# An H3 block with a feed-forward on one core: other pairs in seven products, another order of units, and odd butterflies first

## The chip, the cores and the metric

The kernel runs on one core of one Trainium2 chip. The metric is the device time of one execution in microseconds (us). For the kernel before, three runs gave a median of 1280.16 us (1279.25 to 1280.81). A matmul runs on PE (TensorE), element-wise work on DVE (VectorE) and ACT (ScalarE), DMAs are issued from the queues of SP (SyncE) and POOL (GpSimd).

## The reference

With q of 2048 x 1024 (S x D), w1 of 1024 x 3584 and w2 of 3584 x 1024 (D x F, F x D), all f32:

```
xn = layernorm(q)
kv = shift_conv(k, shift_k) * v                # short causal conv, 4 taps per channel
y  = irfft(rfft(kv) * rfft(ssm_k))[:2048]      # per channel, long causal conv
y  = y + kv * ssm_D
out = q + xn * y + silu(xn @ w1) @ w2
```

## The kernel before, in words

**Two matmuls of the feed-forward.** GEMM1 makes h = silu(xn @ w1), GEMM2 makes h @ w2. All operands are f16 halves, a high part and a low part of an f32 value, and a product is three matmuls for each 128 of the contraction: high by high, high by low, low by high (`steps`, L926 to L928, and `steps2`, L1054 to L1056). Splitting a value is `split` (L357): ACT writes the high part (L347), then DVE the low part (L339).

**Pairs and units.** F is cut into 14 pairs of two 128-wide column tiles. The rows of x are cut into four blocks of 512: two row halves, `sp` 0 and 1, of two blocks each. A unit is one pair and one row half. GEMM1 makes pairs 0 and 1 of the first half in the ordinary way (`plain_unit`), and every other unit by seven products instead of eight (`PRODUCTS`, L42: P1 to P7, in the order P1, P7, P6, P2, P5, P3, P4, with the next unit's P1 ahead of P3). The operands of these products are sums of blocks of x (A11, S1, ...) and of w1 (B11, T1, ...). `units` (L962) lists the units: pairs 2 to 13 of the first half, then pairs 0 to 13 of the second.

**The factors.** `factors_w1` makes the w1 operands of each pair from raw w1 by splits and DVE sums, into halves of six tiles called wo. For pairs 2 to 13 it also stores them to DRAM (`spill_w1`, tensors ws), and `load_factors` brings them back for the second half. Pairs 0 and 1 are made last, for the second half alone. `load_x` brings the x operands of the second half with transposing DMAs on SP's queue (L329) from xsp, one for each operand, as soon as the last unit of the first half has used the operand before it (`product` sets that token at pair NP - 1, the last unit of each half).

**Evacuation.** `evacuate` copies and adds the products of a unit with ACT and DVE into two row blocks, in f32, in halves of three tiles called hf, and `silu` runs on ACT. In a plain pair, `blocks` (L851) splits each row block into f16 parts in a tile ht and stores them to hs. For the pairs in `PAIRS` (10 to 13) GEMM2 uses seven products too: `quad` (L809) makes from the two row blocks seven operands, with four DVE sums of 128x512 and splits of 128x1024 (three) and 128x512 (one) and seven stores to hsf (names A.. and S..). The upper block of such a pair lies in place x4 (`room`, `parts`), the lower one in hf. There are two ht tiles.

**GEMM2.** For each of two column halves and sixteen row tiles, five chunks of four plain column tiles (`PLAIN`, L45), then `units2` with seven products for the four pairs of `PAIRS`. The w2 operands are prepared in `norms_w2`, and `load_w2` lists the loads. All operands of h come from DRAM (`load_h`).

**The long convolution.** Per group of 128 channels (eight groups) the transform is done in two stages: `stage1` does matmuls for eight residues t in four steps (`TO`, order 1, 3, 0, 2), `to_spec` (L1496) turns each step's result into a sum and a difference, `forward` (L1511) does butterflies on DVE over all eight, `product` multiplies by the filter, and stages back follow. `transforms` (L1630) runs forward for a group when steps 0 and 1 of `spec` (even and odd t) are both complete.

**What sets the order.** The program has one queue of instructions per engine. `Order` (L106) is a planner: generators yield operations with a cost and a bias, and at each step the one with the earliest due time less bias is put out. The engines then run their own lists in that order, and each waits where its next instruction's operands aren't there.

Of the kernel before, what the change touches and what calls it, by code (L numbers as in the profile page):

```python
# [13 lines left out]
F16 = mybir.dt.float16  # L14
# [25 lines left out]
            "P5": ("S1", "T1"), "P3": ("S4", "B22"), "P4": ("A22", "T4")}  # L40
XPLACE = dict(A11=2, A12=3, A22=5, S1=0, S2=6, S3=7, S4=1)

PAIRS = (10, 11, 12, 13)
NQ = len(PAIRS)
PLAIN = [j for j in range(NF) if j // 2 not in PAIRS]  # L45
NC = len(PLAIN) // 4
# [242 lines left out]
def h3_ffn_kernel(ctx, tc, x, kp, vs, fs, shift, dskip, w1, w2, cfwd, cinv, out):  # L289
# [75 lines left out]
    dram = ctx.enter_context(tc.tile_pool(name="dram", bufs=1, space=bass.MemoryType.DRAM))  # L365
    hsf = [{p[0]: dram.tile([4, P, NQ, 2, P], F16, name=f"hsf{p[0]}{b}") for p in PRODUCTS.values()} for b in range(2)]
    hs = [dram.tile([4, P, NF, 2, P], F16, name=f"hs{b}") for b in range(4)]
    ws = {i: {n: dram.tile([P, 2, KH, len(n) * P], F16, name=f"ws{i}_{n[0]}") for n in FACTORS} for i in range(2, NP)}
    xsp = {p[0]: dram.tile([P, 4, KH, 2, P], F16, name=f"xsp{p[0]}") for p in PRODUCTS.values()}

    ps_ff = ctx.enter_context(tc.tile_pool(name="ps_ff", bufs=1, space=bass.MemoryType.PSUM))
# [373 lines left out]
    def factors_w1():  # L745
        for n, (kind, i) in enumerate(pairs):
            yield (0.21, 0.15, 0.1, 0.05)[min(n, 3)]
            yield flag["scaled", n]
            hv, toks, _ = raws[n]
            b = {(a, j): hv[a][:, :, j * P:(j + 1) * P] for a in range(2) for j in range(2)}  # L750
            if kind == "plain":
                for j in range(2):
                    if i == 0:
                        yield (0.21, 0.18)[j]
                    for a in range(2):
                        yield from w_part(("plain", i, a, j), b[a, j], i)
                toks[0].set()
                continue
            sp = 0 if i > 1 else 1
            keep = ws.get(i, defaultdict(lambda: None))  # L760

            def part(names, src):
                spill = keep[names] is not None
                o, tok = yield from w_place(len(names), 1 + spill)
                yield from split(o[:, 0], o[:, 1], src, wsc[:, i, 0:1])
                factors_there(sp, i, names, o, tok)
                if spill:
                    spills.append((keep[names], o, tok, len(names)))
            yield from part(("B11",), b[0, 0])
            yield t1_r.ready  # L770
            t1, t1k = t1_r.tile([P, KH, P])
            yield v_tt(t1, b[0, 1], b[0, 0], SUB)
            yield v_tt(b[0, 1], b[1, 1], b[0, 1], SUB)
            yield v_tt(b[0, 0], b[0, 1], b[0, 0], ADD)
            yield from part(("T2", "T3"), hv[0])
            yield from part(("B21", "B22"), hv[1])
            yield from part(("T1",), t1)
            t1k.set()
            yield v_tt(b[1, 0], b[1, 0], b[0, 0], SUB)
            toks[0].set()  # L780
            yield from part(("T4",), b[1, 0])
            toks[1].set()
        flag["w done"].set()
        flag["spills end"].set()
# [10 lines left out]
                tok.set()  # L795

    def load_factors():
        for i in range(2, NP):
            for names in FACTORS:
                o, tok = yield from w_place(len(names))  # L800
                yield L(o, ws[i][names])
                factors_there(1, i, names, o, tok)
        flag["factors"].set()
# [148 lines left out]
    def product(n, i, sp, o, first=False):  # L952
        xname, wname = PRODUCTS[n]
        yield flag["w", sp, i, wname]
        yield flag["x", sp, xname]
        w, tok = wops[sp, i, wname]
        yield from steps(o, w, xo[sp][xname], first, True, not first)
        tok.set()
        if i == NP - 1:
            xtok[sp][xname].set()  # L960

    def units():  # L962

        todo = [(i, 0) for i in range(2, NP)] + [(i, 1) for i in range(NP)]
        yield ff.ready
        one = ff.tile([P, 4, P])
        yield from product("P1", *todo[0], one[0], True)
        for n, (i, sp) in enumerate(todo):
            if sp == 1:
                flag["unit", i].set()  # L970
                flag["room", 1].set()
            if i in PAIRS:
                add(quad(i, sp), 0.1)
            made, seen = defaultdict(Token), defaultdict(Token)
            yield ff.ready
            c = ff.tile([P, 4, P])
            add(evacuate(i, 2 * sp, one, c, made, seen), EB)
            yield from product("P7", i, sp, c[0], True)
            yield seen["P1"]
            two = seen["bank"][0]  # L980
            yield from product("P6", i, sp, two)
            made["P6"].set()
            yield from product("P2", i, sp, one[0])
            made["P2"].set()
            yield seen["P6"]
            yield from product("P5", i, sp, two)
            made["P5"].set()
            if n + 1 < len(todo):
                yield ff.ready
                one = ff.tile([P, 4, P])  # L990
                yield from product("P1", *todo[n + 1], one[0], True)
            yield seen["P5"]
            yield from product("P3", i, sp, two)
            made["P3"].set()
            yield seen["P7"]
            yield from product("P4", i, sp, c[0])
            made["P4"].set()
# [330 lines left out]
    def convolution(floor):  # L1328
# [130 lines left out]
        def stage1():  # L1459

            for g in range(NG):
# [4 lines left out]
                for t in TO:  # L1466
                    yield flag["part", g, t]
                    (hi, htok), (lo, ltok) = part.pop((g, t))
                    two = []
                    for i in range(2):  # L1470
                        for c in range(2):
                            if i == 0:
                                yield lambda: ps_r.ready() or spare()
                                ps, tok = (ps_r if ps_r.ready() else ff).tile([P, 2, 2 * P])
                                two.append((ps, Token(), Token(), Token()))
                                diff = (tmp[:, :, t // 2] if t % 2 else sp[:, :, 5 + t])[:, :, c]
                                add(to_spec(g, t, sp[:, :, t, c, :], diff, *two[c], tok), CB)
                            ps, seen, made = two[c][:3]
                            if i == 1:
                                yield seen  # L1480

                            def mm():
                                cf = cfw[:, t + 4 * i, :, c * P:(c + 1) * P]
                                kw = dict(skip_group_check=i == 1)
                                nc.tensor.matmul(ps, cf[:, 0], hi[:, i], start=i == 0, stop=False, **kw)
                                nc.tensor.matmul(ps, cf[:, 0], lo[:, i], start=False, stop=False, **kw)
                                nc.tensor.matmul(ps, cf[:, 1], hi[:, i], start=False, stop=True, **kw)
                            yield T(mm, ps, [hi[:, i], lo[:, i]], 0.65, m=1.0)
                            (made if i else two[c][3]).set()
                    htok.set()  # L1490
                    ltok.set()
# [4 lines left out]
        def to_spec(g, t, total, diff, ps, seen, made, half, tok):  # L1496

            yield half
            if g > 0:
                yield flag["taken", g - 1, t]  # L1500
                if t % 2 == 0:
                    yield flag["taken", g - 1, t + 1]
            yield a_act(diff, ps, AF.Copy, 2.0)
            seen.set()
            yield made
# [5 lines left out]
        def forward(g):  # L1511
# [16 lines left out]
            def I2(a, step):  # L1528
                return C(a, 2, step)[:, :, :, 1, :]

            yield v_tt(C(4, 2, 2), C(0, 2), C(2, 2), SUB)
            yield v_tt(C(2, 2), C(0, 2), C(2, 2), ADD)
            yield v_tt(C(0), C(2), C(3), ADD)
            yield v_tt(C(1), C(2), C(3), SUB)
            yield v_tt(pair(R(2), I(3)), pair(R(4), I(4)), pair(I(6), R(6)), ADD)
            yield v_tt(pair(I(2), R(3)), pair(I(4), R(4)), pair(R(6), I(6)), SUB)
            yield v_tt(pair(R(4), I(6)), pair(R(5), I(5)), pair(I(7), R(7)), ADD)
            yield v_tt(pair(I(4), R(6)), pair(I(5), R(5)), pair(R(7), I(7)), SUB)
            yield v_tt(R2(5, 2), R2(8, 1), I2(8, 1), ADD)
            yield v_tt(I2(5, 2), I2(8, 1), R2(8, 1), SUB)  # L1540
            yield v_tt(pair(R(8), R(9)), pair(R(5), I(5)), pair(I(7), R(7)), ADD)
            yield v_tt(pair(I(8), I(9)), pair(I(5), I(7)), pair(R(7), R(5)), SUB)
            for o, s, t, r in ((5, 8, 4, RT), (4, 8, 4, -RT), (7, 9, 6, RT), (6, 9, 6, -RT)):
                flat = [C(a)[:, :, 0].rearrange("p s c w -> p s (c w)") for a in (o, s, t)]
                yield v_stt(flat[0], flat[1], r, flat[2], MUL, ADD)
            tok.set()
# [82 lines left out]

        def transforms():  # L1630
            for g in range(NG):
                yield flag["spec", g, 0]
                yield flag["spec", g, 1]
                yield from forward(g)
                yield from product(g)
                add(result_scales(g), CB)
                yield from inverse(g)
# [173 lines left out]
```

## Time and profile before

| quantity | before |
|---|---|
| median of three runs | 1280.16 us |
| span of the profiled execution | 1279.8 us |
| PE busy | 1244.7 us (97%) |
| DVE busy | 1146.4 us (90%) |
| ACT busy | 725.5 us (57%) |
| POOL busy | 133.0 us (10%) |
| DMA, mean | 222 GB/s |

The profile is of one execution of 17054 instructions, whose own span is the second row; the page gives no other time for it. The share of an engine is its busy time over that span. Matmuls on PE are pipelined, so their durations overlap, and a step of time in the kernel is read from the starts. Where an engine is idle, the row says whose work it waited for. Positions are in us from the start of the span: GEMM1 ends near 613, the convolution's last DVE work is at about 1256.

### The profile page before, as it was taken

To read this page: it belongs to the slowest core of one execution; us is meant where nothing else is said; L and a number is where in the kernel's file an instruction comes from. 1 tells how busy PE (TensorE), PEld (TensorE's weight loads), DVE (VectorE), ACT (ScalarE), POOL (GpSimd) and SP (SyncE) were. 2 spreads that over 40 slices of the span, in tenths; PEclk is the share of its full clock that TensorE was granted. 3 is DMA by queue.
4 is the path that set the end of the run, shared out by engine and by line. 5 is a ranking of instruction groups with operands and counts; after the bars stand their busy time and mean duration, and the time that the engine had idled before them with its cause. 6 is when DMAs were issued, how large, how long until landed. Compare 5 with 4: busy or idle time off the path is not lost. (4 is left out here: it accounts for less than half of the span.)

```text
span 1279.8 us, 17054 instructions
## 1 busy us (share of the span) xinstructions
PE 1244.7 (97%) x6082; PEld 604.2 (47%) x6082; DVE 1146.4 (90%) x1521; ACT 725.5 (57%) x1153; POOL 133.0 (10%) x141
## 2 busy tenths in 40 slices
PE   7899999989899999999999999999999999999997
PEld 6444444434344544445444544544454454445443
DVE  8999997889699969999899899899979989997991
ACT  6858896768566687559652632553253274445231
POOL 0000000000000020002010310210030030113223
PEclk9899999989999999999999999999999999999999
DMA  9447899889999899669995684598486487877766
GB/s 329 157 150 237 284 321 307 269 241 248 290 365 356 277 282 334 225 197 261 351 290 125 138 226 111 124 254 266 107 189 180 113 170 225 228 148 142 158 127 92
DMA packets 247988, 284.53 MB, mean 222 GB/s; under 512 B 43744, under 2 KB 162528, under 8 KB 246624
## 3 DMA queue, kind: packets, MB, share of 16 engines
q1 hardware_dynamic: 221168, 258.54, 63.6%
q0 software_dynamic: 26736, 24.92, 14.6%
q8 instruction: 47, 0.77, 0.2%
q14 instruction: 37, 0.30, 0.1%
HBM read 185.88 MB, written 98.57 MB: 222 GB/s over the span
## 5 line engine op out<-in xcount | busy, mean ns | idle before, releaser
L1054 PE MATMUL ff<-x,wo 128*128 128x512 f16 x864 | 327.4, 379 | 1.4 <-ACT hf L347 1.0
L1056 PE MATMUL ff<-x,wo 128*128 128x512 f16 x864 | 327.4, 379 | 0.0
L1055 PE MATMUL ff<-x,wo 128*128 128x512 f16 x864 | 327.4, 379 | 0.0
L926 PE MATMUL ff<-x,wo 128*128 128x512 f16 (+1 forms) x808 | 306.1, 379 | 8.6 <-ACT hf L347 3.8
L927 PE MATMUL ff<-x,wo 128*128 128x512 f16 (+1 forms) x808 | 306.0, 379 | 2.6 <-DVE x L339 2.6
L928 PE MATMUL ff<-x,wo 128*128 128x512 f16 (+1 forms) x808 | 306.0, 379 | 2.5 <-DVE wo L339 2.4
L336 DVE TENSOR_TENSOR spec<-spec 128x512 f32<-128x512 f32 (+2 forms) x256 | 260.6, 1053 | 2.8 <-DVE spec L336 0.5
L1056 PEld LDWEIGHTS <-wo 128*128 128x128 f16 x864 | 84.5, 98 | 101.9
L1055 PEld LDWEIGHTS <-wo 128*128 128x128 f16 x864 | 84.5, 98 | 100.8 <-issue 2.4
L1054 PEld LDWEIGHTS <-wo 128*128 128x128 f16 x864 | 85.4, 99 | 98.7
L928 PEld LDWEIGHTS <-wo 128*128 128x128 f16 x808 | 79.7, 99 | 101.8 <-issue 5.8
L926 PEld LDWEIGHTS <-wo 128*128 128x128 f16 x808 | 81.4, 101 | 92.2 <-ACT wo L347 3.4
L927 PEld LDWEIGHTS <-wo 128*128 128x128 f16 x808 | 79.7, 99 | 95.6 <-issue 9.1
L347 ACT ACTIVATE hf<-ff,invc 128x512 f32<-128x512 f32 x64 | 43.5, 680 | 118.9 <-PE ff L1056 86.8
L333 POOL DMA_DIRECT2D out<-yt x64 | 74.5, 1362 | 338.5 <-DVE yt L339 220.9
L333 POOL DMA_DIRECT2D out<-hf x63 | 57.4, 911 | 457.9 <-ACT hf L347 391.8
L336 DVE TENSOR_TENSOR tmp<-spec 128x2048 f32<-128x2048 f32 (+1 forms) x48 | 92.5, 1933 | 1.0
L347 ACT ACTIVATE spec<-spec 128x1024 bf16<-128x1024 f32 x32 | 33.8, 1055 | 86.1 <-DVE spec L336 86.0
L339 DVE SCALAR_TENSOR_TENSOR ht<-hf,wsc,ht 128x1024 f16<-128x1024 f32 (+1 forms) x56 | 67.3, 1204 | 13.7 <-ACT ht L347 13.7
L347 ACT ACTIVATE ht<-hf,wsc 128x1024 f16<-128x1024 f32 (+1 forms) x56 | 60.5, 1083 | 11.4 <-DMA hsfS<-ht 6.9
L339 DVE SCALAR_TENSOR_TENSOR wo<-raw,wsc,wo 128x512 f16<-128x512 f32 (+1 forms) x56 | 56.1, 1012 | 9.0 <-ACT wo L347 9.0
L339 DVE SCALAR_TENSOR_TENSOR acc<-kin,taps,acc 128x1024 f32<-128x1024 f32 x48 | 61.4, 1280 | 2.2 <-ACT acc L347 2.2
(181 smaller groups left out, 1750.1 us busy)
## 6 DMA issues: line engine op xcount, KB each, us to landing
wo<-hs SPq DMA_DIRECT2D x160, 256.0 KB, 3.6
hs<-ht SPq DMA_DIRECT2D x80, 256.0 KB, 5.6
out<-hf POOLq DMA_DIRECT2D x63, 256.0 KB, 4.5
raw<-in_w SPq DMA_DIRECT2D x28, 512.0 KB, 5.8
wraw<-in_w SPq DMA_DIRECT2D x24, 512.0 KB, 6.3
w2n<-in_w SPq DMA_DIRECT2D x24, 512.0 KB, 6.8
kin<-in_kp SPq DMA_DIRECT2D x16, 704.0 KB, 6.1
xt<-in_x SPq DMA_DIRECT2D x16, 512.0 KB, 7.4
```

Source lines behind the costliest of these rows:

```text
L333: return Op("POOL", 1.1, 3.0, lambda: nc.gpsimd.dma_start(o, i, accum_op=ADD), [i], [o], m, n)
L336: return V(lambda: nc.vector.tensor_tensor(o, a, b, op=op), o, [a, b], **k)
L339: return V(lambda: nc.vector.scalar_tensor_tensor(o, a, s, b, op0=op0, op1=op1), o, [a, b] + ([] if isinstance(s, float) else [s]), **k)
L347: nc.scalar.activation(o, i, func, scale=scale, **kw)
L926: nc.tensor.matmul(o, w[:, 0, k], xf[:, :, k, 0], start=first and k == 0, stop=False, **kw)
L927: nc.tensor.matmul(o, w[:, 0, k], xf[:, :, k, 1], start=False, stop=False, **kw)
L928: nc.tensor.matmul(o, w[:, 1, k], xf[:, :, k, 0], start=False, stop=last and k == KH - 1, **kw)
L1054: nc.tensor.matmul(po, hx[:, n, 0, :], wc[:, n, 0, :], start=first and n == 0, stop=False, **kw)
L1055: nc.tensor.matmul(po, hx[:, n, 0, :], wc[:, n, 1, :], start=False, stop=False, **kw)
L1056: nc.tensor.matmul(po, hx[:, n, 1, :], wc[:, n, 0, :], start=False, stop=last and n == 3, **kw)
```

## The change

Three things are changed. First, `PAIRS` are 8 to 11 instead of 10 to 13, so that pairs 12 and 13 are plain. Second, the units come from a list `UNITS`: the first half has pairs 2 to 13 as before, the second begins with pair 13, then 0, 1, 2 to 12. Pair 13's factors are made once, are not stored to DRAM, and stay in wo until the second half's unit has used them; the loads of factors therefore start at pair 2 and end at 12. Tokens that stood at the last pair of a half now stand at the last of `UNITS[sp]`, and the flags "unit" are numbered by place in the second half. Third, in a convolution group the four butterflies on odd t come first, when the odd steps are complete, and the butterflies on even t wait for the even ones; the tiles that hold the differences are shifted by one place so that an even step no longer needs two places of the group before.

```diff
-PAIRS = (10, 11, 12, 13)
+PAIRS = (8, 9, 10, 11)
+UNITS = [[*range(2, NP)], [NP - 1, 0, 1, *range(2, NP - 1)]]
...
-    ws = {... for i in range(2, NP)}
+    ws = {... for i in range(2, NP - 1)}
...
             def part(names, src):
                 spill = keep[names] is not None
-                o, tok = yield from w_place(len(names), 1 + spill)
+                both = i == NP - 1
+                o, tok = yield from w_place(len(names), 1 + spill + both)
                 yield from split(o[:, 0], o[:, 1], src, wsc[:, i, 0:1])
                 factors_there(sp, i, names, o, tok)
+                if both:
+                    factors_there(1, i, names, o, tok)
...
     def load_factors():
-        for i in range(2, NP):
+        for i in UNITS[1][3:]:
...
     def product(n, i, sp, o, first=False):
...
-        if i == NP - 1:
+        if i == UNITS[sp][-1]:
             xtok[sp][xname].set()
...
     def units():
-        todo = [(i, 0) for i in range(2, NP)] + [(i, 1) for i in range(NP)]
+        todo = [(i, sp) for sp in range(2) for i in UNITS[sp]]
...
-                flag["unit", i].set()
+                flag["unit", n - len(UNITS[0])].set()
...
-                                diff = (tmp[:, :, t // 2] if t % 2 else sp[:, :, 5 + t])[:, :, c]
+                                diff = (tmp[:, :, t // 2] if t % 2 else sp[:, :, 4 + t])[:, :, c]
...
         def to_spec(g, t, total, diff, ps, seen, made, half, tok):
             yield half
             if g > 0:
                 yield flag["taken", g - 1, t]
-                if t % 2 == 0:
-                    yield flag["taken", g - 1, t + 1]
...
         def forward(g):
...
-            yield v_tt(C(4, 2, 2), C(0, 2), C(2, 2), SUB)
-            yield v_tt(C(2, 2), C(0, 2), C(2, 2), ADD)
-            yield v_tt(C(0), C(2), C(3), ADD)
-            yield v_tt(C(1), C(2), C(3), SUB)
-            yield v_tt(pair(R(2), I(3)), pair(R(4), I(4)), pair(I(6), R(6)), ADD)
-            yield v_tt(pair(I(2), R(3)), pair(I(4), R(4)), pair(R(6), I(6)), SUB)
-            yield v_tt(pair(R(4), I(6)), pair(R(5), I(5)), pair(I(7), R(7)), ADD)
-            yield v_tt(pair(I(4), R(6)), pair(I(5), R(5)), pair(R(7), I(7)), SUB)
+            yield flag["spec", g, 1]
             yield v_tt(R2(5, 2), R2(8, 1), I2(8, 1), ADD)
             yield v_tt(I2(5, 2), I2(8, 1), R2(8, 1), SUB)
             yield v_tt(pair(R(8), R(9)), pair(R(5), I(5)), pair(I(7), R(7)), ADD)
             yield v_tt(pair(I(8), I(9)), pair(I(5), I(7)), pair(R(7), R(5)), SUB)
-            for o, s, t, r in ((5, 8, 4, RT), (4, 8, 4, -RT), (7, 9, 6, RT), (6, 9, 6, -RT)):
+            yield flag["spec", g, 0]
+            yield v_tt(C(5, 2, 2), C(0, 2), C(2, 2), SUB)
+            yield v_tt(C(2, 2), C(0, 2), C(2, 2), ADD)
+            yield v_tt(C(0), C(2), C(3), ADD)
+            yield v_tt(C(1), C(2), C(3), SUB)
+            yield v_tt(pair(R(2), I(3)), pair(R(5), I(5)), pair(I(7), R(7)), ADD)
+            yield v_tt(pair(I(2), R(3)), pair(I(5), R(5)), pair(R(7), I(7)), SUB)
+            yield v_tt(pair(R(5), I(7)), pair(R(4), I(4)), pair(I(6), R(6)), ADD)
+            yield v_tt(pair(I(5), R(7)), pair(I(4), R(4)), pair(R(6), I(6)), SUB)
+            for o, s, t, r in ((4, 8, 5, -RT), (5, 8, 5, RT), (6, 9, 7, -RT), (7, 9, 7, RT)):
...
         def transforms():
             for g in range(NG):
-                yield flag["spec", g, 0]
-                yield flag["spec", g, 1]
                 yield from forward(g)
```

More of the change, by code (lines that the diff above doesn't have):

```diff
@@ L367, in h3_ffn_kernel @@
     hs = [dram.tile([4, P, NF, 2, P], F16, name=f"hs{b}") for b in range(4)]
-    ws = {i: {n: dram.tile([P, 2, KH, len(n) * P], F16, name=f"ws{i}_{n[0]}") for n in FACTORS} for i in range(2, NP)}
+    ws = {i: {n: dram.tile([P, 2, KH, len(n) * P], F16, name=f"ws{i}_{n[0]}") for n in FACTORS} for i in range(2, NP - 1)}
     xsp = {p[0]: dram.tile([P, 4, KH, 2, P], F16, name=f"xsp{p[0]}") for p in PRODUCTS.values()}
```

## The prediction

> **What bounds the kernel now.** First the page's list of engines and the table by stretches of 32 us (columns: wall time, then busy time and instructions of PE, PEld, DVE, ACT, POOL, then the granted clock, DMA share, GB/s).
>
> ```profile
> PE 1244.7 (97%) x6082; PEld 604.2 (47%) x6082; DVE 1146.4 (90%) x1521; ACT 725.5 (57%) x1153; POOL 133.0 (10%) x141
> ```
> ```profile
> 192.00:224.00 32.00, 32.00 (x152) 14.59 (x150) 25.17 (x36) 22.02 (x30) 0.95 (x1) 1.00 0.90 307
> 224.00:256.00 32.00, 30.64 (x144) 13.79 (x143) 25.68 (x42) 25.48 (x39) 0.00 (x0) 1.00 0.81 269
> 256.00:288.00 32.00, 28.40 (x123) 12.50 (x122) 28.15 (x46) 20.90 (x30) 0.00 (x0) 0.89 0.81 241
> 288.00:320.00 32.00, 31.63 (x152) 14.93 (x151) 29.30 (x41) 26.40 (x39) 0.00 (x0) 1.00 1.06 248
> 320.00:352.00 32.00, 27.51 (x119) 11.87 (x117) 22.25 (x24) 16.43 (x27) 0.76 (x1) 0.95 1.04 290
> 352.00:384.00 32.00, 30.28 (x141) 13.67 (x140) 31.00 (x29) 21.65 (x37) 0.00 (x0) 1.00 1.06 366
> ...
> 1248.00:1280.00 32.00, 22.70 (x117) 11.14 (x114) 5.08 (x7) 4.02 (x6) 11.03 (x11) 0.94 0.67 91
> ```
> ```profile
> 384.00:704.00 320.00, 320.00 (x1561) 153.56 (x1559) 297.65 (x360) 206.94 (x328) 24.61 (x24) 1.00 0.87 270
> 704.00:1248.00 544.00, 542.12 (x2686) 264.29 (x2685) 501.88 (x587) 234.04 (x400) 94.90 (x98) 1.00 0.70 171
> ```
>
> PE is busy all of 384 to 704 and 542.12 of the 544 us behind it, while DVE works 297.65 of 320 and 501.88 of 544: near the bound, but not it. From 384 on only the end can be won. Matmuls, ACT and DVE instructions keep their numbers under the change, so the time moves only by stalls of PE. They lie in 224 to 384: idle 1.36, 3.60, 0.37, 4.49 and 1.72 us (32 less PE busy), and where the granted clock is 0.89 and 0.95, another 0.11 and 0.05 of 32 us, 3.5 and 1.6. So the first half's end (224 to 288) loses about 8.5 us, and the second half's start (288 to 384) 8.2.
>
> Whom PE waited for between 224 and 384, and the matmuls at the longest wait:
>
> ```profile
> PE ff L926 <- ACT hf L347: 3.8, 2, 2.9
> PE ff L926 <- ACT wo L347: 2.9, 1, 2.9
> PE ff L928 <- DVE wo L339: 2.0, 3, 0.7
> PE ff L926 <- DVE hf L336: 1.7, 1, 1.7
> ```
> ```profile
> 272.23 0.38 PE L927 MATMUL ff<-x,wo 128*128 128x512 f16 x1
> ...
> 273.09 0.38 PE L928 MATMUL ff<-x,wo 128*128 128x512 f16 x1
> 276.37 0.61 PE L926 MATMUL ff<-x,wo 128*128 128x512 f16 x1 [2.90 <-ACT wo L347]
> 276.77 0.63 PE L927 MATMUL ff<-x,wo 128*128 128x512 f16 x1
> ```
>
> The wait on wo is pair 13's first factor, which comes late. Behind it a matmul takes 0.61 to 0.63 us where one took 0.38, and starts lie 0.40 apart (276.37 to 276.77) instead of 0.215 (the four from 272.23 to 273.09); at 0.215 a product of twelve matmuls takes 2.6. The wait of 2.9 on hf is an evacuation, and its cause stands in ACT's and SP's rows:
>
> ```profile
> 315.49 0.59 ACT L347 ACTIVATE ff<-ff 128x512 f32<-128x512 f32 x1
> ...
> 318.76 1.14 ACT L347 ACTIVATE wo<-raw,wsc 128x1024 f16<-128x1024 f32 x1
> 324.64 0.72 ACT L347 ACTIVATE ht<-hf,wsc 128x512 f16<-128x512 f32 x1 [4.74 <-DMA hsfS<-ht]
> ```
> ```profile
> 282.98 4.70 SPq L329 DMA_TRANSPOSE x<-xspA  x1
> 287.77 0.53 SPq L324 DMA_DIRECT2D ws_T<-wo  x1
> ...
> 302.13 6.57 SPq L329 DMA_TRANSPOSE x<-xspS  x1
> 308.79 1.08 SPq L324 DMA_DIRECT2D hsfS<-ht  x2
> 309.97 5.81 SPq L329 DMA_TRANSPOSE x<-xspA  x1
> 315.88 4.55 SPq L329 DMA_TRANSPOSE x<-xspS  x1
> 320.52 1.08 SPq L324 DMA_DIRECT2D hsfS<-ht  x2
> 321.69 6.12 SPq L329 DMA_TRANSPOSE x<-xspS  x1
> ...
> 329.08 5.48 SPq L329 DMA_TRANSPOSE x<-xspA  x1
> ```
>
> These are seven transposing loads of x from 282.98 to 334.56 (the last starts at 329.08), four of xspS and three of xspA, each holding SP for 4.55 to 6.57 us, with fifteen other transfers among them, nine of these hsf stores. The stores that would free an ht tile stand behind two of them (309.97 to 320.52), ACT stops 4.74 us at the next split, and PE's evacuation is queued behind that split.
>
> **The change part by part.** All DVE prices come from these groups of 196 to 384 (mean ns after the busy time):
>
> ```profile
> L339 DVE SCALAR_TENSOR_TENSOR ht<-hf,wsc,ht 128x1024 f16<-128x1024 f32 x12 | 15.4, 1281 | 7.5 <-ACT ht L347 7.5
> L339 DVE SCALAR_TENSOR_TENSOR acc<-kin,taps,acc 128x1024 f32<-128x1024 f32 x12 | 15.3, 1279 | 0.0
> L336 DVE TENSOR_TENSOR hf<-ff,hf 128x512 f32<-128x512 f32 x18 | 12.3, 685 | 0.1
> L336 DVE TENSOR_TENSOR x<-hf,x 128x512 f32<-128x512 f32 x4 | 2.8, 688 | 0.0
> L339 DVE SCALAR_TENSOR_TENSOR ht<-hf,wsc,ht 128x512 f16<-128x512 f32 x4 | 3.0, 751 | 4.2 <-ACT ht L347 4.2
> ```
>
> *1. Pairs 8 to 11 as quads, first half.* A quad costs DVE three splits of 1.281, one of 0.751 and four sums of 0.688: 7.35 us. A plain pair costs two splits, 2.56. In before's order, quads 10 and 11 (and 12) stand among the last factors; now 8, 9, 10 and 11 do. Ahead of pair 13's factors DVE thus gets two quads more, 2 x 4.79 = 9.6 us. DVE's idle time in 192 to 256 was 64 − 50.85 = 13.15 us, nominally enough. But half of it, by my estimate, is forced: DVE waits there for products that PE has yet to make and can do nothing early. Bounds: 0 (all hidden) to +9.6 (none). If 6.6 us are usable, 3.0 are late. Against this, the small waits on DVE's wo (2.0 in three) move: one at pair 11 goes, pair 12's grows. I take +1.5, nearer to 0, because the old loss of 8.5 already holds one such wait with its clock loss, and the new lateness adds to it rather than making a new one.
>
> *2. Second half starts with pair 13.* In the changed order the seven transposes have two loads of raw, four hs stores and one kf load among them; in before, the fifteen named above. The five stores of ws13 and their loads go:
>
> ```profile
> ws_T<-wo SPq DMA_DIRECT2D x24, 256.0 KB, 5.1
> wo<-ws_T SPq DMA_DIRECT2D x24, 256.0 KB, 7.3
> ```
>
> A store held SP for 0.53 us (287.77). They feed no instruction that PE waits for, so removed they are worth nothing themselves. What counts is the 8.2 us: with no quad store behind a transpose, ACT's 4.74 us stop has no cause. Units 13 and 0 are plain, and their four hs stores can still stand behind a transpose of up to 6.57 us, but there are two ht tiles and a plain pair takes only two splits per unit where a quad takes four. I leave 1.5 us of the 8.2 (a wait of the 1.72 kind, without clock loss): −6.7. Bounds: 0 (the transposes hold whatever store comes) to −8.2. The cost: pair 13's factors stay in wo through another 18 us (seven products of 2.6 us). Pair 0's are needed by the same 18 us later, so this nearly cancels; T4 of pair 0 waits for the wo tile that P6 of pair 13 frees, and comes close: 0 to +1, inside the bounds.
>
> *3. Second half ends with a plain pair behind a quad.* Order on DVE from the last quad's first sums on: four sums, S3/S1's split, S2/S4's split, the gate's acc, two splits of w2, and only then the last unit's evacuation of P5 into a half of hf, for which P4 of pair 12 waits. hf has three wholes; the lower block's whole is released by the S3/S1 split. That list is 4 x 0.688 + 4 x 1.281 + 1.279 + 0.685 = 9.84 us. PE does in the same time P5 (it is at work when the list starts, some 1.6 us of it left by my estimate), the copy out (0.59, as ACT's ff<-ff copies) and P3 (2.6). P3 waits about 1.0 with no next P1 to cover the copy, P4 is due 1.6 + 1.0 + 2.6 = 5.2 us in, and would wait up to 4.6; I take 3.3, since DVE in 384 to 704 ran with 22.35 us idle and can be somewhat ahead. Behind GEMM2's start one norm of the gate, whose sums queue behind this list, I price at 1.7 (0 to 2.8). Sum +6.0. Bounds: 0 (before's row has PE busy 320 of 320) to +9.8.
>
> *4. Odd butterflies alone.* The four wide subtractions and sums on even indices no longer hold the four odd ones: DVE starts sooner in each of eight groups. DVE's waits there:
>
> ```profile
> DVE spec L336 <- ACT spec L347: 30.3, 16, 3.9
> ```
>
> At most 30.3 us of DVE waiting go, 3.8 a group. But PE, not DVE, is full from 384 on (1.88 us idle in 704 to 1248), so I take 0. Bounds: −1.9 to +1.9: ACT's to_spec copies compete with evacuations either way.
>
> *5. Tail.* The last unit2 starts when the weights and products are there, as before; DVE is busy 5.08 of the last 32 us, so an earlier conv end brings nothing: 0.
>
> Sum: +1.5 − 6.7 + 6.0 + 0 + 0 = +0.8 on the execution's span of 1279.8, 1280.6. The runs' median (1280.16) is 0.36 above that span: **1281.0**.
>
> On the clock one rule bears on new waits. The Trainium skill, "TensorE: Matmul & The Clock Gate", Part 1, says that PE falls to half clock after an idle window of about 3.4 us and needs about as long a busy one to come back. By this trace a wait of 2.90 us is already enough, and that of 1.72 us was not (352 to 384 kept 1.00). By that rule none of the waits that I take for the changed kernel (3.3 at most) would cost clock, and the sum stays; by the trace it may not, which is rival C.
>
> **The rivals.**
> *A, the gain stays:* new work in 1 and 3 hides in DVE's idle 13.15 and 22.35 us. For: those idle sums are larger than 9.6 and 9.84. Against: DVE's idle comes in waits, not in one piece. Time: 1281.0 − 1.5 − 6.0 = 1273.5; with the whole 8.2 gone, 1272.0.
> *B, slower: the quad list ahead of the last plain unit and ahead of pair 12's factor holds PE for 3 us or more each.* Price: 3 at its 4.6 + 1.0 + 2.8 = 8.4, and 1 at 3.0 + one more spell at half clock (3.5, as in 256 to 288): 6.5. With −6.7: +8.2, 1288.4. It decides once DVE runs level with PE, without a lead of over 2 us, when each list starts. For: DVE busy 29.30 and 31.00 of 32 around such quads. Against: 320 to 352 had 9.75 idle.
> *C, the clock alone:* sizes as in the forecast, but each wait of 2.9 or more (3.3 in part 3, pair 12's about 3) brings a spell of half clock: 1.6 to 3.5 each by the rows of 320 and 256. Time: 1281.0 + 1.6 to 7.0, about 1284.6. For: the wait of 2.90 us was followed by half clock both times. Against: it takes waits in one piece, and those of part 3 may come in two.
> *D, part 2 doesn't do it:* hs stores stand behind the transposes as hsf's did, 8.2 stays: 1281.0 + 6.7 = 1287.7.
>
> **How the numbers follow.** Runs tell 0.2%, about 2.6 us, from no change: faster is below 1277.6, slower above 1282.7. Forecast (the terms nearly cancel, own range 1277 to 1285): 0.40, of it 0.06 faster, 0.20 same, 0.14 slower. A: 0.25, faster. B: 0.17, C: 0.10, D: 0.08, slower but for 0.02 of C. So faster 0.31, same 0.22, slower 0.47. The range 1272 to 1288 leaves out A's lower edge and B's and D's upper.
>
> **What would show it.** Part 1: PE's wait for ACT wo near 276 stays near 3 us, one near 257 appears. Part 2: in 288 to 384 the granted clock stays 1.00 and "ACT ht <- DMA hsf" is gone there. Part 3: PE waits for DVE hf between 600 and 640. Part 4: fewer us of DVE spec <- ACT spec, and no change of PE in 704 to 1248. Wrong would be: PE full in 600 to 640 (then A), a long wait in 288 to 384 (then D), or a clock below 1.00 at a third place (then C).

## The result and the profile after

| | before | after |
|---|---|---|
| median of ten runs, us | 1280.11 (1279.25 to 1281.08) | 1283.23 (1281.69 to 1285.12) |
| span of the profiled execution, us | 1279.8 | 1281.7 |
| ratio, 95% interval | | 1.0026 (1.0016 to 1.0035) |

The changed kernel is slower by 0.26%, 3.1 us. The parts are much larger than this sum. The table by stretches of the changed kernel (wall time, then busy time and instructions of PE, PEld, DVE, ACT, POOL, then granted clock, DMA share, GB/s) stands beside that of before:

```profile
224.00:256.00 32.00, 29.33 (x139) 13.32 (x138) 30.07 (x50) 27.17 (x41) 0.00 (x0) 1.00 0.92 299
256.00:288.00 32.00, 27.43 (x117) 11.82 (x115) 29.09 (x46) 20.26 (x29) 0.00 (x0) 0.89 0.81 241
288.00:320.00 32.00, 32.00 (x158) 15.59 (x156) 26.28 (x33) 24.96 (x37) 0.00 (x0) 1.00 1.06 244
320.00:352.00 32.00, 32.00 (x150) 14.46 (x148) 29.08 (x31) 20.54 (x32) 0.76 (x1) 1.00 0.83 220
352.00:384.00 32.00, 31.84 (x154) 15.08 (x153) 31.55 (x38) 23.95 (x41) 0.00 (x0) 1.00 1.04 363
384.00:576.00 192.00, 191.49 (x947) 93.07 (x946) 182.24 (x228) 137.41 (x221) 14.18 (x13) 1.00 0.88 275
576.00:608.00 32.00, 28.54 (x138) 13.34 (x137) 30.85 (x31) 24.41 (x39) 5.25 (x5) 1.00 0.99 283
608.00:640.00 32.00, 28.84 (x128) 12.79 (x128) 31.00 (x36) 19.39 (x31) 0.00 (x0) 0.95 0.98 317
640.00:704.00 64.00, 63.06 (x323) 31.77 (x322) 60.65 (x72) 32.98 (x53) 7.79 (x9) 1.00 0.64 171
704.00:1248.00 544.00, 542.09 (x2674) 262.81 (x2672) 481.39 (x563) 219.55 (x377) 97.39 (x101) 1.00 0.72 174
```

What PE lost in each stretch, in us, is counted for every kernel below as for the prediction: wall time less PE's busy time, and the part of the clock that wasn't granted. The rows of 384 to 704 of before show 0.

| stretch | before | after | change | prediction |
|---|---|---|---|---|
| 224 to 288, end of the first half | 8.5 | 10.8 | +2.3 | +1.5 |
| 288 to 384, start of the second | 8.2 | 0.2 | −8.0 | −6.7 |
| 384 to 576 | 0 | 0.5 | +0.5 | 0 |
| 576 to 640, end of GEMM1 | 0 | 8.2 | +8.2 | +6.0, for the whole end |
| 640 to 704 | 0 | 0.9 | +0.9 | |
| 704 to 1248, GEMM2 | 1.9 | 1.9 | 0 | 0 |

The sum is +3.9; the two spans differ by 1.9, since the clock is given in hundredths, half-speed matmuls overlap, and the executions differ by about 1 us in their first 64 us too. The waits of PE in the changed kernel, over the whole span, are these (total, times, longest):

```profile
PE ff L932 <- DVE wo L340: 4.6, 3, 2.6
PE ff L930 <- DVE hf L337: 4.4, 2, 3.9
...
PE ff L930 <- ACT wo L348: 2.7, 1, 2.7
...
PE ff L1059 <- DVE x L340: 1.9, 1, 1.9
```

The wait on ACT wo is still pair 13's first factor. The one of 2.6 on DVE wo is new, pair 12's, at 252. The wait of 2.9 on an evacuation has gone from 324, and one of 3.9 stands at the end of GEMM1: P4 of pair 12 waits for DVE's sum in hf. DVE's list ahead of that sum and PE's two waits, in order of time:

```profile
599.85 0.68 DVE L337 TENSOR_TENSOR hf<-hf 128x512 f32<-128x512 f32 x1
600.45 1.28 DVE L340 SCALAR_TENSOR_TENSOR x<-wraw,tau,x 128x1024 f16<-128x1024 f32 x1
601.64 0.68 DVE L337 TENSOR_TENSOR hf<-x,hf 128x512 f32<-128x512 f32 x1
602.25 1.27 DVE L340 SCALAR_TENSOR_TENSOR x<-w2n,tau,x 128x1024 f16<-128x1024 f32 x1
603.44 0.68 DVE L337 TENSOR_TENSOR x<-hf,x 128x512 f32<-128x512 f32 x1
604.16 0.69 DVE L337 TENSOR_TENSOR x<-x 128x512 f32<-128x512 f32 x1
604.77 1.28 DVE L340 SCALAR_TENSOR_TENSOR ht<-hf,wsc,ht 128x1024 f16<-128x1024 f32 x1
605.96 1.28 DVE L340 SCALAR_TENSOR_TENSOR acc<-kin,taps,acc 128x1024 f32<-128x1024 f32 x1
607.16 1.28 DVE L340 SCALAR_TENSOR_TENSOR ht<-x,wsc,ht 128x1024 f16<-128x1024 f32 x1
608.35 0.68 DVE L337 TENSOR_TENSOR hf<-ff,hf 128x512 f32<-128x512 f32 x1
```
```profile
602.47 0.38 PE L930 MATMUL ff<-x,wo 128*128 128x512 f16 x1 [0.69 <-ACT hf L348]
...
609.09 0.58 PE L930 MATMUL ff<-x,wo 128*128 128x512 f16 x1 [3.87 <-DVE hf L337]
```

Here is the list that the prediction added up: four sums and two splits of the last quad, with w2's splits and a step of the gate among them, then the evacuation. It takes 599.85 to 609.03, 9.2 us (estimated 9.84). P3 starts 2.6 us into it, just as the forecast had it (1.6 us of P5 left, then a wait of 1.0), so P4 comes 3.87 us too late, and its first matmuls run at half clock (0.58 to 0.63 us a matmul). The list is full without a gap: DVE is behind, it doesn't wait. On SP no store of quad operands stands among the transposing loads any more:

```profile
303.52 1.08 SPq L325 DMA_DIRECT2D hs<-ht  x2
304.69 5.21 SPq L330 DMA_TRANSPOSE x<-xspA  x1
310.00 4.85 SPq L330 DMA_TRANSPOSE x<-xspS  x1
```

### The profile page after: what moved, and what is told of

Its sections match the earlier page's. It is cut to its first block, busy times and chain, and to the rows that moved or that the text cites. A ratio compares the mean times of both kernels' runs of the same rounds, so it can differ in the third digit from the quotient of the medians.

```text
span 1281.7 us, 17018 instructions
## 1 busy us (share of the span) xinstructions
PE 1242.7 (97%) x6082; PEld 603.3 (47%) x6082; DVE 1144.8 (89%) x1521; ACT 725.9 (57%) x1153; POOL 133.0 (10%) x141
## 4 chain that ended last, share of the span: by engine, by line
PE 59%; DVE 22%; issue 7%; DMA 7%; ACT 4%; POOL 1%; SPq 0%; POOLq 0%; DVEq 0%; ACTq 0%
PE ff L932 9%; PE ff L930 9%; PE ff L931 9%; PE ff L1058 7%; PE ff L1060 7%; PE ff L1059 7%; DVE spec L337 6%; DVE tmp L337 3%; DVE acc L340 2%; DVE x L340 2%; PE ps L1489 2%; DVE wo L340 2%; PE ps L1491 2%; PE ps L1490 2%; DVE ht L340 1%
## 5 line engine op out<-in xcount | busy, mean ns | idle before, releaser
L334 POOL DMA_DIRECT2D out<-yt x64 | 71.7, 1346 | 349.0 <-DVE yt L340 225.3
L348 ACT ACTIVATE spec<-ps 128x512 f32<-128x512 f32 x84 | 48.7, 590 | 24.0 <-PE ps L1491 22.4
L337 DVE TENSOR_TENSOR spec<-tmp 128x512 f32<-128x512 f32 (+1 forms) x80 | 61.0, 793 | 0.8
```

Of the source, the lines that this page charges most:

```text
L334: return Op("POOL", 1.1, 3.0, lambda: nc.gpsimd.dma_start(o, i, accum_op=ADD), [i], [o], m, n)
L337: return V(lambda: nc.vector.tensor_tensor(o, a, b, op=op), o, [a, b], **k)
L348: nc.scalar.activation(o, i, func, scale=scale, **kw)
```

## The experiments

The theory after the result was that the three parts do what the stretches suggest: the pairs alone remove 288 to 384, and a plain pair behind the last quad costs the end of GEMM1. Each run below is set beside runs of before on its chip; times are medians in us.

**Each part alone, and the change without its butterflies.** E1 has only this edit:

```diff
-PAIRS = (10, 11, 12, 13)
+PAIRS = (8, 9, 10, 11)
```

> Only the pairs that take seven products are changed (8 to 11); units and butterflies as before. Theory: the 9 us that went between 288 and 384 went because no store of quad operands stands behind the transposing loads any more, and that comes from the pairs alone; the first half's end costs 2 more, and near 575 to 613 two plain pairs stand behind the last quad, for 3 to 9 us. Sum -4 to +2 on before: 1276 to 1282, with granted clock 1.00 in 288 to 384 and no ACT wait on hsf there. Rival (the order of units and the kept factors gave the 9): the loss of 8 to 9 us in 288 to 384 stays, sum +5 to +11: 1285 to 1291.

Measured: 1309.6, ratio 1.0234 (1.022 to 1.0248). Both expectations are missed. The stretch of 288 to 384 loses 0.8, 8.6 + 3.5 (clock 0.89) and 0: 12.9 us, but not by quad stores. ACT's row shows why, and PE's stretches at both places:

```profile
341.11 1.06 ACT L347 ACTIVATE wraw<-wraw 128x1024 f32<-128x1024 f32 x1 [9.47 <-DMA wraw<-in_w]
```
```profile
320.00:352.00 32.00, 23.45 (x99) 10.00 (x98) 14.40 (x18) 17.57 (x30) 0.76 (x1) 0.89 1.01 289
...
576.00:608.00 32.00, 25.76 (x118) 11.97 (x117) 31.72 (x41) 20.00 (x27) 0.00 (x0) 0.93 0.66 208
608.00:640.00 32.00, 19.30 (x95) 10.33 (x94) 24.77 (x28) 24.94 (x39) 9.71 (x9) 0.82 1.00 253
```

A load of w2, put on SP's queue behind the last transposing load, arrives late, and ACT stands 9.47 us in front of its square with the conv copies queued behind. The end of GEMM1 loses 6.2 + 2.2 and 12.7 + 5.8, 26.9 us, a loss that only E11 reaches again. PE's longest waits there are 6.2 us of a convolution matmul for ACT and 6.7 us of GEMM1 for a DVE sum in hf. The butterflies of before are in this kernel, so such a loss doesn't need those of the change. No run takes it apart, and its cause is open.

E2 is the order of units and the kept factors alone:

```diff
+UNITS = [[*range(2, NP)], [NP - 1, 0, 1, *range(2, NP - 1)]]
...
+                if both:
+                    factors_there(1, i, names, o, tok)
```

> Only the order of units is changed, with pair 13's factors kept; pairs 10 to 13 take seven products and the butterflies are as before. Theory: quads 12 and 13 still store among the transposing loads, so 288 to 384 loses 6 to 10 us as before, and the end of GEMM1 has a quad last and loses nothing: 1279 to 1283. Rival (the order of units gave the gain): 288 to 384 loses under 2 us, 1270 to 1273. Second rival (the new order costs at the end of GEMM1 whatever the pairs): 4 us or more lost in 576 to 640, 1284 to 1289.

Measured: 1286.46, ratio 1.0051 (1.0038 to 1.0065). ACT's waits between 280 and 384, and a stretch of PE:

```profile
ACT ht L348 <- DMA hsfA<-ht: 8.6, 2, 5.7
```
```profile
288.00:320.00 32.00, 30.90 (x150) 14.73 (x148) 24.08 (x33) 23.48 (x36) 0.00 (x0) 1.00 1.05 230
320.00:352.00 32.00, 27.68 (x120) 12.18 (x120) 25.51 (x30) 19.21 (x27) 0.76 (x1) 0.95 0.86 223
352.00:384.00 32.00, 30.68 (x142) 13.69 (x140) 28.81 (x30) 18.56 (x31) 0.00 (x0) 1.00 0.91 307
```

The start of the second half loses 1.1 + 4.3 + 1.3 + 1.6 = 8.3, as before, with ACT behind hsf stores (another 4.7 us behind those of S operands): the theory's half of this is right, the order of units alone wins nothing there. The second rival is right as well, though: the end of GEMM1 loses 1.1 + 4.1 us with a quad last, and the time is over the theory's 1283. So the two parts win the 8 us only together: the pairs take the quad stores out from among the transposing loads, and with the order of units the loads that ACT needs next come later. The first load of w2 is issued at 335.39 in E1, right behind the transposing loads, and at 347.75 in the changed kernel, where ACT's longest wait for such a load between 280 and 384 is 2.5 us and PE's waits come to 0.2.

E3 is the changed kernel with the `forward`, `to_spec` and `transforms` of before.

> The change without its butterflies: pairs 8 to 11 and the new order of units, butterflies as before. Theory: the 8.6 us lost in 576 to 640 come from the plain pair behind the quad and stay; some 1 us of small waits of stage1's matmuls in 640 to 1248 goes: 1281 to 1283.5. Rival (the butterflies that begin sooner crowd DVE at the end of GEMM1): 3 us or less lost in 576 to 640, 1275 to 1278.

Measured: 1278.27, ratio 0.9984 (0.9975 to 0.9992), faster than before and 5.0 us below the changed kernel. The rival is right about the end of GEMM1 (0.6 us lost), where the theory falls; its time is missed by 0.3. The rows of E3, PE's stretches first, then DVE's list (its first and last) and PE's first matmul of the same P3:

```profile
576.00:608.00 32.00, 31.74 (x170) 16.57 (x169) 31.90 (x36) 26.48 (x36) 4.39 (x4) 1.00 0.99 276
608.00:640.00 32.00, 31.62 (x154) 14.77 (x153) 28.16 (x26) 22.50 (x38) 7.03 (x7) 1.00 1.04 309
704.00:1248.00 544.00, 537.02 (x2668) 262.29 (x2667) 496.02 (x579) 233.83 (x400) 97.13 (x100) 1.00 0.71 170
```
```profile
582.34 0.69 DVE L337 TENSOR_TENSOR hf<-hf 128x512 f32<-128x512 f32 x1
...
590.86 0.68 DVE L337 TENSOR_TENSOR hf<-ff,hf 128x512 f32<-128x512 f32 x1
```
```profile
589.12 0.38 PE L930 MATMUL ff<-x,wo 128*128 128x512 f16 x1 [0.26 <-ACT hf L348]
```

The plain pair stands behind the quad here too, and the list is as long (582.34 to 591.54, 9.2 us), but it starts 6.8 us ahead of P3 instead of 2.6, and P4, which follows 2.6 us behind P3's start, doesn't wait: the sum is there 0.2 us ahead of it. What differs is DVE's lead, the time by which its list starts ahead of the product on PE. The butterflies of the change also do something in GEMM2: without them 704 to 1248 loses 7.0 us, with them 1.9. Of the 7.6 us that they cost at the end of GEMM1 they give 5.1 back. These sums are of one execution each; the two profiled ones differ by 3.3 us, the medians by 5.0.

E4 is the butterflies alone, in the kernel before.

> Only the butterflies are changed. Theory: PE is the bound behind 384, so within 1.5 us of before: 1279 to 1282, PE losing 9 us again in 288 to 384 and under 0.5 in 576 to 640. Rival (they crowd DVE): 3 us or more lost in 576 to 640, 1283 to 1289. Second rival (they shorten the convolution and with it the end): 1276 or less.

Measured: 1293.26, ratio 1.0106 (1.0087 to 1.0124). None of the three: the end of GEMM1 loses only 1.9 (608 to 640), but the stretches behind it lose:

```profile
640.00:704.00 64.00, 61.47 (x294) 28.73 (x293) 63.13 (x70) 27.08 (x42) 4.76 (x6) 1.00 0.73 201
704.00:1248.00 544.00, 537.99 (x2677) 262.84 (x2676) 488.30 (x572) 229.88 (x398) 99.42 (x102) 1.00 0.72 173
```

2.5 in 640 to 704 and 6.0 in 704 to 1248. The same butterflies that spare GEMM2 5 us beside the new pairs and units cost it 4 beside the old ones. Why is open.

**Is it the plain pair, or DVE's lead?** E5 leaves the changed kernel's work as it is and puts the quads' work of the second half ahead in the planner's order:

```diff
+    QB = (0.1, 1.0)
...
-        add(factors(("S3", "S1"), flat[1], (ltok,)), 0.1)
+        add(factors(("S3", "S1"), flat[1], (ltok,)), QB[sp])
...
-        add(factors(("S2", "S4"), flat[0], (utok, flag["quads", sp])), 0.1)
+        add(factors(("S2", "S4"), flat[0], (utok, flag["quads", sp])), QB[sp])
...
-                add(quad(i, sp), 0.1)
+                add(quad(i, sp), QB[sp])
```

> The changed kernel, in whose second half alone the quads' work goes ahead of other work in the order (bias 1.0 instead of 0.1). Theory of DVE's lead: the 8.6 us in 576 to 640 are lost because the last quad's sums and splits stand on DVE behind convolution work that the butterflies brought forward; put ahead, under 2 us are lost there and the time is 1274 to 1278. Rival (a plain pair behind a quad costs it whatever stands ahead): 5 us or more stay, 1281 to 1284.

Measured: 1272.23, ratio 0.9932 (0.9919 to 0.9946). The theory of the lead holds, and the gain is larger than it said:

```profile
576.00:608.00 32.00, 32.00 (x170) 16.53 (x169) 30.43 (x37) 28.61 (x44) 7.17 (x7) 1.00 0.96 271
608.00:640.00 32.00, 32.00 (x150) 14.52 (x149) 31.90 (x28) 20.24 (x32) 4.23 (x5) 1.00 1.06 331
704.00:1248.00 544.00, 543.55 (x2693) 264.93 (x2692) 487.89 (x571) 227.21 (x390) 101.84 (x105) 1.00 0.71 173
```

PE loses nothing from 576 to 640 and 0.45 in GEMM2, with the same work on every engine. The last quad's sums now start at 586.95, 13.5 us ahead of P3 (600.41), and the sum that P4 needs is done at 600.40, 4.5 us ahead of P4 (604.94). E6 tries the rival directly, with pair 12 put ahead of the quads:

```diff
-UNITS = [[*range(2, NP)], [NP - 1, 0, 1, *range(2, NP - 1)]]
+UNITS = [[*range(2, NP)], [NP - 1, 0, 1, *range(2, 8), 12, *range(8, 12)]]
```

> The changed kernel, with pair 12 placed behind pair 7 in the second half, so that it ends with the quads 8 to 11 and no plain pair stands behind a quad there. Rival of e5 (a plain pair behind a quad is the cause): under 1.5 us lost in 576 to 640, 1274 to 1277. Theory of DVE's lead: the lack of lead meets the last quads instead, 4 to 7 us stay, 1279 to 1283.

Measured: 1282.84, ratio 1.0019 (1.001 to 1.0027). The rival falls:

```profile
576.00:608.00 32.00, 29.77 (x131) 13.08 (x130) 31.90 (x33) 26.92 (x44) 3.05 (x3) 0.95 1.08 324
608.00:640.00 32.00, 30.17 (x143) 13.92 (x142) 31.79 (x37) 16.84 (x21) 1.57 (x2) 1.00 0.99 312
```

2.2 + 1.6 + 1.8 = 5.7 us stay in 576 to 640 with no plain pair behind a quad. So a plain pair isn't needed for a loss of this size. That DVE's lead is the cause here too isn't shown: the wait of 2.2 is for ACT's copy into hf, and only the 1.8 are waits for DVE, for an operand of GEMM2. E7 is E5's edit with the butterflies of before.

> As the kernel with the quads' work first, but with the butterflies of before. Theory: once the end of GEMM1 has its lead, the butterflies are worth nothing either way, since PE is the bound: within 2 us of the kernel with the quads first, 1274 to 1278. Rival (they cost in GEMM2 too, or they gain there): 4 us or more apart.

Measured: 1275.32, ratio 0.9964 (0.9951 to 0.9976), 3.1 above E5: more than the theory's 2, less than the rival's 4, and it is the butterflies of the change that gain. In its profiled execution (1278.69 us), PE loses 2.0 in 576 to 640, 1.0 in 640 to 704 and 2.9 in 704 to 1248 (541.15 of 544 busy). With the quads' work first, the butterflies of the change are thus worth some 3 us.

**The end of the first half.** E8 adds to E5 an earlier place for the last factors:

```diff
-            yield (0.21, 0.15, 0.1, 0.05)[min(n, 3)]
+            yield (0.21, 0.15, 0.1, 0.05)[min(n, 3)] if n < 12 else 0.1
```

> As the kernel with the quads' work first, and in the first half the factors of pairs 12 and 13 (and of 0 and 1) get the bias of the quads (0.1 instead of 0.05). Theory: the 10.5 us lost in 224 to 288 are factors that stand on DVE behind the quads' work; with the same bias the wait of 2.7 us for pair 13's first factor and the half clock behind it go, 3 to 6 us: 1269 to 1273. Rival (the factors are late for the scales or the raw loads, not for DVE's order): within 1.5 us of the kernel with the quads first.

Measured: 1278.31, ratio 0.9986 (0.9975 to 0.9998), 6.1 above E5: both times are missed. The theory's mechanism is there, and the gain is lost at the next place:

```profile
256.00:288.00 32.00, 29.77 (x132) 13.18 (x133) 31.44 (x50) 22.63 (x33) 0.00 (x0) 0.95 0.84 243
...
320.00:352.00 32.00, 27.02 (x124) 11.95 (x123) 26.27 (x29) 16.83 (x25) 0.76 (x1) 1.00 0.74 179
```
```profile
338.70 1.06 ACT L348 ACTIVATE hi<-kf 128x1024 bf16<-128x1024 f32 x1 [7.01 <-DMA kf<-in_dskip]
```

224 to 288 loses 1.4 + 2.2 + 1.6 = 5.2 instead of E5's 10.8, but the load of kf now stands behind the last transposing load instead of ahead of two, and ACT waits 7.01 us for it. 288 to 352 loses 6.1 where E5 loses nothing, and 704 to 1248 loses 3.0 where E5 loses 0.45. E9 takes E5 and moves the quads of the first half instead, `QB = (0.2, 1.0)`.

> As the kernel with the quads' work first in the second half (bias 1.0), and in the first half with a bias of 0.2 instead of 0.1. Theory: the first half's 10.7 us in 224 to 288 are the order of quads and factors on DVE; with the quads of pairs 8 and 9 done in DVE's idle time ahead of 256, pair 13's first factor is less late, no half clock follows, and 3 to 6 us go: 1266 to 1270. Rival (the work of two more quads has to fit, whatever its order): the waits only move within 224 to 288, 1271 to 1275.

Measured: 1270.26, ratio 0.9917 (0.9903 to 0.993), the fastest of all, between the theory's range and the rival's.

```profile
224.00:256.00 32.00, 30.09 (x144) 13.77 (x142) 30.11 (x48) 25.64 (x38) 0.00 (x0) 1.00 0.94 299
256.00:288.00 32.00, 32.00 (x151) 14.51 (x150) 30.71 (x42) 25.11 (x36) 0.00 (x0) 1.00 0.93 261
288.00:320.00 32.00, 29.40 (x144) 14.13 (x143) 22.42 (x36) 20.41 (x32) 0.00 (x0) 1.00 1.07 246
```

1.9 us are lost in 224 to 288 instead of 10.8, and no half clock follows. 2.6 come back in 288 to 320, where PE now waits for the x operands themselves (1.4 and 1.2), and 704 to 1248 loses 3.2.

**Two controls.** E10 has E5's edit in the kernel before.

> The kernel before with nothing but the quads' work of the second half ahead of other work (bias 1.0). Theory: before loses nothing in 576 to 640 and its 8.2 to 9.5 us in 288 to 384 come from quad stores behind transposing loads, so nothing is won: 1278 to 1282. Rival (the order of the quads alone gives what the changed kernel with it has won): 1272 to 1276.

Measured: 1286.26, ratio 1.0041 (1.0028 to 1.0053). The rival falls: the order of the quads gains nothing by itself, it is even slower than the theory said. Its profiled execution (1283.28 us) loses 4.2 + 1.6 (clock 0.95) in 320 to 352, as before does, and more than before in 576 to 608 (1.0 instead of 0) and in GEMM2 (4.4 instead of 1.9).

E11 is E1 with the first w2 loads held back by one unit (`yield flag["unit", 1]` at the head of `squares_w2`).

> As the kernel with the pairs alone changed, but the loads of w2 for its norms begin one unit later, at the start of pair 1's unit in the second half. Theory: in the kernel with the pairs alone, the 12.5 us in 288 to 352 are ACT's 9.5 us wait at a square of w2, whose load stands on SP behind the transposing loads, and that is what the new order of units moves 18 us away; here that wait is gone and 288 to 352 loses under 6 us. Rival (the wait at the transposing loads themselves, which only the order of units eases): 9 us or more stay.

Measured, one run: 1307.23 beside 1282.06 for before. The wait for w2 is gone and another has taken its place:

```profile
ACT xg L347 <- DMA xg<-in_x: 9.1, 1, 9.1
```
```profile
320.00:352.00 32.00, 24.20 (x106) 10.76 (x106) 13.38 (x17) 15.90 (x30) 0.76 (x1) 0.95 1.00 278
```

288 to 384 loses 0.1 + 7.8 + 1.6 = 9.5: the theory's number is missed, and the rival's "9 or more" met. Holding w2's load back isn't enough: xg's load, which then stands behind the transposing ones on SP and is the next that ACT wants, takes its place. The end of GEMM1 loses as much as in E1 (27.0 us by the same sum).

## Why the prediction was right or wrong

The time (1283.23 beside 1281.0, range 1272 to 1288) and the likeliest sign (slower, 0.47) were right, by terms that cancel as forecast and for reasons that were partly not the right ones. That the sum came so near is in part luck: the largest term has the right size, and not the cause that it was given (3 and 4 below).

1. *Pairs 8 to 11 in the first half, +1.5:* measured +2.3. Pair 12's first wait grew to 2.61 us at 252, as foreseen. E8 and E9 show that it is the order on DVE, not the amount of work: with the quads a little earlier the same two quads more cost nothing there (1.9 us lost in place of before's 8.5), though 2.6 come back behind 288.
2. *The start of the second half, −6.7:* measured −8.0, the whole loss. "With no quad store behind a transpose, ACT's 4.74 us stop has no cause" was right for the store, and incomplete. E1 takes the quad stores out and loses 12.9, E11 9.5, since then w2's or xg's load is the one behind the transposes. E2 leaves them in and loses 8.3. Both parts of the change are needed. The five ws13 stores, priced at nothing, were not tried alone.
3. *The end of GEMM1, +6.0:* measured +8.2, and 0.9 behind it. The chain is the one forecast: the list starts 2.6 us ahead of P3 (taken 1.6 + 1.0), P3 waits 0.69 (taken 1.0), P4 3.87 (taken 3.3), half clock behind it costs 1.6 (rival C's price), and GEMM2's first wait is 1.9 us for a w2 operand split on DVE (taken 1.7, for a norm). But a plain pair behind a quad isn't by itself the cause: E3 has that list and a loss of 0.6, E6 has no such pair and a loss of 5.7. The start of the list was right as a number. The step that failed is its source: the prediction took this start for what the order of units brings. With the butterflies of before the same list starts 6.8 us ahead of P3 (E3), and with the quads' work put first the last quad's sums start 13.5 us ahead (E5). The condition named under rival B, DVE's lead on PE, decides it, and what took the lead away are the butterflies, which the prediction priced at nothing. That +6.0 is near +8.2 is luck.
4. *The butterflies, 0 within ±1.9:* wrong, and the largest error. PE is the bound in total, and still E3, the changed kernel without them, is 5.0 us faster. The prediction counted what a shorter DVE chain saves at the end of the span; it left out that DVE's work which starts sooner in GEMM1 stands ahead of evacuations there. DVE works 182.24 us in 384 to 576 and 176.61 in before. This fits E3, where it works 171.97. But E4 and E7 show that the effect isn't a constant of the butterflies: beside before's pairs and units they cost 13 us, with the quads' work first they are worth 3. Why their effect in GEMM2 changes its sign is open.
5. *The tail, 0:* right; the convolution's last DVE work ends at 1211 instead of 1256, and the end doesn't follow.

Rival A's time (1273.5) is what the same change gives when DVE's order is mended (E5, 1272.23). Rival C did happen at one of its places; its "about 1284.6" isn't worked out from its bounds, whose middle is 1285.3. Rival D is refuted: four hs stores do stand among the transposing loads, and 288 to 384 loses 0.2. E2's 8.3 stay behind hsf stores, which isn't what D said.

## What to carry to other kernels

An engine that is busy for 90% of the span and isn't the bound, as DVE here, can still have no slack to give away at the places where it feeds the bound: ask how far ahead of the bound it is there, not how idle it is on average, and give the work that the bound waits for its place in the order before adding work that can wait. Where transfers that hold a queue for 5 us each are issued in a row, look at every load and store behind them and at who stands in front of it; taking one away brings up the next. Parts of a change that touch one order aren't additive: the three here measured +2.3%, +0.5% and +1.1% alone and +0.26% together, and a change that loses can hold a gain of 0.8%.

## What was not expected of the hardware

A wait of PE doesn't decide by its length alone whether half clock follows. That of 2.90 us in before and that of 3.87 us in the changed kernel are followed at once by matmuls of 0.58 to 0.63 us. In the changed kernel that of 2.61 us isn't (the matmuls behind it stay at 0.38 to 0.39 us), that of 2.72 us is followed by a matmul of 0.39 us and by half clock only behind a second wait of 1.73 us. In E10 a wait of 2.90 us, as long as that in before and at the same place of the kernel, is followed by matmuls of 0.38 to 0.39 us, and half clock comes only behind a second wait of 1.13 us. In E6 one of 2.23 us is followed by three matmuls of 0.38 to 0.39 us and then by half clock, and in E8 one of 3.41 us has no half clock behind it:

```profile
340.00 0.38 PE L933 MATMUL ff<-x,wo 128*128 128x512 f16 x1
343.78 0.38 PE L931 MATMUL ff<-x,wo 128*128 128x512 f16 x1 [3.41 <-ACT ff L348]
```

The Trainium skill, "TensorE: Matmul & The Clock Gate", Part 1, says that the gate looks at windows of about 3.4 us that run freely. That a wait of 3.41 us can pass and one of 2.90 not, and that two waits of 2.90 us end differently, agrees with windows that begin at times of their own. That a wait shorter than a window can be enough isn't what the page's rule says, and here the measurement decides; no run shows where the windows begin.
